# Fewer small routing steps on VectorE, placed only in the last two rounds of a top-k search, and GpSimd's row scaling ahead of its transfers

## The chip, the cores and the metric

The kernel runs on one core of one Trainium2 chip. The metric is the device time of that core in microseconds, from start to end of one execution; lower is better. The comparisons below use the median of several executions.

## The reference

Two blocks follow each other. The first is attention with 8 batches, 8 heads, 576 positions and 64 dimensions a head: of each row of scores only those not below the row's 32nd largest are kept. Its output is 4,608 tokens of 512 values. The second block sends each token to the one of 8 experts with the largest gate logit, runs it through that expert's two matrices (512 to 1,024, ReLU, 1,024 to 512) and scales it by the gate's probability.

```python
scores = scale * np.matmul(q, k.transpose(0, 1, 3, 2))
kth = np.partition(scores, -top_k, axis=-1)[..., -top_k:-top_k + 1]     # top_k = 32
attn = softmax(np.where(scores >= kth, scores, -1e9))
x = (attn @ v)                      # then (B,H,S,D) -> (B*S, H*D)
logits = x @ w_gate
expert_idx = np.argmax(logits, axis=1)
probs = softmax(logits)             # gate_w: the chosen expert's share
h = np.maximum(x_sorted[lo:hi] @ w1[e], 0.0)    # per expert e, tokens sorted by expert
y_sorted[lo:hi] = h @ w2[e]
out = gate_w[:, None] * y
```

## The kernel before, in words

**Attention.** A unit is two heads of one batch (u = 0 to 3), so a batch has four units. The work list has 144 steps, 18 a batch; each handles two tiles of 128 query rows against all 576 keys. One step goes through the engines in this way: TensorE multiplies queries and keys (line 292); ACT copies the scores from PSUM (L299); VectorE folds them in halves (L306, L308, and L314, L316 for the second fold) and searches for the 32 largest in four rounds, each of which takes the eight largest of either tile (MAX8, L354) and, but for the last, strikes them out (MATCH_REPLACE8, L362); ACT turns the 32nd largest into a bound (L371) and computes from it how far each score lies below it (L387); GpSimd subtracts that from the scores (L396, two instructions of 128x576 a step) and records doubts about the folding (L377); ACT takes the exponentials (L404); TensorE transposes the weights and multiplies by the values (L415 to L452). VectorE works on step i+1 while GpSimd subtracts for step i. A small instruction `nbias` (L358) on GpSimd follows round 0 of each search.

**After a unit** its output is brought into token order. The generator `ending` does that in pieces at named places of the loop. ACT forms divisors and VectorE their reciprocals (L481). At the place "rows" GpSimd multiplies the gate's partial logits (L489), adds them up (L491, L492, L494) and scales the rows (L502, 128x640).

**Routing** follows the last unit of a batch, while the next batch's attention runs. `choice` finds each token's expert (L512 to L522); TensorE counts the tokens before each (L533 to L536) and ACT copies the running count `run` (L1093); `places` turns that into row numbers `posi` and gate weights (L548 to L558); five indirect transfers on GpSimd's queue scatter the rows to DRAM (L569), one a step; `table` works out which experts have filled a block of 128 rows and lists the new blocks for the loader (L613 to L653). After batch 0, `filled_up` runs before `table`; in the last batch another table, `end_table`, and halves of blocks follow.

**The small steps of VectorE.** `choice`, `places`, `table` and the reciprocals are generators on a list `aside`. The search calls `tick()` between its instructions, and each call runs one small step:

```python
for m in m_all:
    nc.vector.max(out=tops[:, m, r * 8:(r + 1) * 8], in_=src[m])
    if r:
        tick()
```

The same stands behind each MATCH_REPLACE8, so rounds 1 and 2 have four places, round 3 has two. What is left on the list when the loop reaches a given place is run there in one go by `through`.

**Expert blocks** are cut in pieces of a few matmuls (L916, L933) that TensorE runs between the attention's products at a planned rate; ACT evacuates them (L813, L921, L942), and GpSimd's queue writes the results out by indirect transfers (`put_rows`, L831), collected in `stores`. A few blocks are kept back until attention has ended; the last ones (L852 to L892) need the last table.

**What sets the order.** TensorE, ACT and VectorE run in the order in which the program writes them. GpSimd's and SyncE's instructions are ordered by the scheduler that builds the kernel, from its own estimates, except that instructions put by `in_turn` keep their order among themselves; a scatter is also tied behind the last GpSimd instruction of the step that issued it. In each step of the loop, the scatter and the stores are issued just behind the subtraction and the doubts, before the places "pool", "relu" and "rows".

Of the kernel before, what the change touches and what calls it, by code (L numbers as in the profile page):

```python
# [9 lines left out]
F32 = mybir.dt.float32  # L10
# [9 lines left out]
NEG = -3.0e38  # L20
STEEP = 2.0 ** 120
EPS = 1e-9


def _ins(ap: bass.AP, axis: int, n: int) -> bass.AP:
# [12 lines left out]
def _inner(ap: bass.AP, n: int) -> bass.AP:  # L38
    return _ins(ap, len(ap.ap), n)
# [3 lines left out]
def kernel(  # L43
# [47 lines left out]
    nc = tc.nc  # L91
# [104 lines left out]
    nc.vector.tensor_copy(e_same, _ins(e_less[:, :], 1, KC))  # L196
    nc.vector.memset(e_same[ST:P, NC, :], 1.0)
    e_at = iota_f("e_at", [P, E], [[CAP, E]])
    slots = iota_f("slots", [1, NSLOT], [[1, NSLOT]])

    def token_ids(t, b):
        return nc.gpsimd.iota(t, pattern=[[P, KC]], base=b * S, channel_multiplier=1)
# [18 lines left out]
    slot_long = slot_last[:, 0, NSLOT + SOON - 3 * E:].rearrange("o (i e) -> o i e", i=3)  # L221
    assert LAST - SURE <= NSLOT + SOON - 3 * E
    done = const.tile([1, E], F32, name="done")
    nc.vector.tensor_scalar_mul(done, e_at[0:1, :], 1.0 / P)
    slot_max = const.tile([1, 3], F32, name="slot_max")
    rare = slot_max[:, 2:3]
    nc.vector.memset(slot_max[:, 0:1], float(E - 1))
    nc.vector.memset(slot_max[:, 1:2], float(EMPTY))
    upto_all = const.tile([1, E + 1], F32, name="upto_all")
    nc.vector.memset(upto_all, 0.0)  # L230
    step_all = const.tile([1, E], F32, name="step_all")
    nc.vector.memset(step_all, float(EMPTY))
# [100 lines left out]
    def search(tiles, s, f, then=lambda: None):  # L333

        m_all = range(2)
        tops = k.small.tile([P, 2, TOP_K], F32, name="tops", bufs=4)
        if k.exact:
            src = [s[:, m, :, :].rearrange("p j k -> p (j k)") for m in m_all]
            width = S
        else:  # L340
            src = [f.few[:, m, 0:QF] for m in m_all]
            width = LW
            for m in m_all:
                for j, away in enumerate((f.l[:, m, :], f.hl[:, m, 0:QF // 2], f.hl[:, m, QF // 2:QF])):
                    nc.vector.max(out=f.few[:, m, QF + 8 * j:QF + 8 * j + 8], in_=away)  # L345
        scr = k.att.tile([P, 2, width], F32, name="scr", bufs=1)
        nbias = k.small.tile([P, 2], F32, name="nbias", bufs=3)
        R = TOP_K // 8

        for r in range(R):  # L350
            if r == R - 1:
                then()
            for m in m_all:
                nc.vector.max(out=tops[:, m, r * 8:(r + 1) * 8], in_=src[m])  # L354
                if r:
                    tick()
            if r == 0:
                in_turn(nc.gpsimd.tensor_scalar_mul(nbias, tops[:, :, 0], -scale))  # L358
            if r < R - 1:
                for m in m_all:  # L360
                    first = r == 0 and not k.exact
                    nc.vector.match_replace(  # L362
                        out=src[m] if first else scr[:, m, :], in_to_replace=tops[:, m, r * 8:(r + 1) * 8],
                        in_values=src[m], imm_value=NEG,
                    )
                    if r:
                        tick()
                    src[m] = f.few[:, m, :] if first else scr[:, m, :]
        thr = tops[:, :, TOP_K - 1]
        low = k.small.tile([P, 2], F32, name="low", bufs=3)  # L370
        nc.scalar.activation(low, thr, AF.Copy, scale=STEEP)  # L371

        def doubts():
            n, i = tiles[0]
            at = n.b * U + n.u
            over = doubt[:, at:at + 2, 2 * NC, :] if tails(tiles) else doubt[:, at, 2 * i:2 * i + 2, :]
            k.last_pool = in_turn(nc.gpsimd.tensor_tensor(  # L377
                over, f.few[:, :, QF + 7:LW:8], _inner(thr, NL), op=ALU.subtract
            )).ins

        return low, nbias, doubts
# [122 lines left out]
    def choice(lg):  # L504
# [6 lines left out]
        def steps():  # L511
            nc.vector.tensor_reduce(mx, lg, axis=AX.X, op=ALU.max)  # L512
            yield
            nc.vector.tensor_tensor(oh, lg, _inner(mx[:, :], E), op=ALU.is_ge)
            yield
            nc.vector.tensor_tensor(oh, oh, _ins(e_less[:, :], 1, KC), op=ALU.mult)
            yield
            nc.vector.tensor_tensor(lg, lg, _inner(mx[:, :], E), op=ALU.subtract)
            yield
            nc.vector.tensor_reduce(idx, oh, axis=AX.X, op=ALU.min)  # L520
            yield
# [18 lines left out]
    def places(r, x):  # L540

        pos = k.small.tile([P, KC, E], F32, name="pos")
        posf = k.small.tile([P, KC], F32, name="posf")
        r.posi = k.small.tile([P, KC], I32, name="posi")
        den = k.small.tile([P, KC], F32, name="den")

        def steps():
# [1 line left out]
            yield  # L549
            nc.vector.tensor_reduce(den, r.lg, axis=AX.X, op=ALU.add)  # L550
            yield
            nc.vector.tensor_reduce(posf, pos, axis=AX.X, op=ALU.add)
            yield
            nc.vector.tensor_scalar_add(den, den, EPS)
            yield
            nc.vector.tensor_copy(r.posi, posf)
            yield
            nc.vector.reciprocal(x[:, :, Dm], den)  # L558
            yield
# [39 lines left out]
    def table(slot_i, n, last, riding=None):  # L599

        sm = k.small
        full = sm.tile([1, E], F32, name="full")
        ci = sm.tile([1, E], I32, name="ci")
        left = sm.tile([1, E], F32, name="left")
        past = sm.tile([1, NSLOT, E], F32, name="past", bufs=1)
        slot_f = sm.tile([1, 2, NSLOT], F32, name="slot_f", bufs=1)
        upto, step = upto_all, step_all

        def steps():
            if last:  # L610
                nc.vector.tensor_scalar_add(full, run[0:1, :], float(P - 1))
                yield
            nc.vector.tensor_copy(ci, full if last else run[0:1, :])  # L613
            yield
            nc.vector.tensor_single_scalar(ci, ci, 7, op=ALU.arith_shift_right)
            yield
            nc.vector.tensor_copy(full, ci)
            yield
            if riding is not None:
                nc.vector.tensor_tensor(full, full, riding, op=ALU.subtract)  # L620
                nc.vector.tensor_tensor(full, full, done, op=ALU.max)
                yield
            nc.vector.tensor_tensor(left, full, done, op=ALU.subtract)
            yield
            nc.vector.tensor_tensor_scan(upto[:, 1:], ones[0:1, 0:E], left, 0.0, op0=ALU.mult, op1=ALU.add)
            yield
            nc.vector.tensor_tensor(step[:, 0:E - 1], done[:, 1:E], full[:, 0:E - 1], op=ALU.subtract)
            yield
            nc.vector.tensor_tensor(
                past[:, 0:n, :], _inner(slots[:, 0:n], E), _ins(upto[:, 1:], 1, n), op=ALU.is_ge  # L630
            )
            yield
            nc.vector.tensor_reduce(slot_f[:, 0, 0:n], past[:, 0:n, :], axis=AX.X, op=ALU.add)
            yield
            nc.vector.tensor_tensor(past[:, 0:n, :], past[:, 0:n, :], _ins(step[:, :], 1, n), op=ALU.mult)
            yield
            nc.vector.tensor_reduce(slot_f[:, 1, 0:n], past[:, 0:n, :], axis=AX.X, op=ALU.add)
            yield
            nc.vector.scalar_tensor_tensor(
                out=slot_f[:, 1, 0:n], in0=slot_f[:, 1, 0:n], scalar=done[:, 0:1], in1=slots[:, 0:n],  # L640
                op0=ALU.add, op1=ALU.add,
            )
            yield
            nc.vector.tensor_tensor(slot_i[:, :, 0:n], slot_f[:, :, 0:n], _inner(slot_max[:, 0:2], n), op=ALU.min)
            yield
            if last:
                nc.vector.tensor_copy(rest_i, upto[:, E:])
            else:
                nc.vector.tensor_scalar_min(upto, upto, float(n))
                yield  # L650
                nc.vector.tensor_tensor(left, upto[:, 1:], upto[:, 0:E], op=ALU.subtract)
                yield
                nc.vector.tensor_tensor(done, done, left, op=ALU.add)  # L653
                yield

        return steps()
# [1 line left out]
    def filled_up():  # L658
# [3 lines left out]
        yield  # L662
        nc.vector.max(out=most, in_=few)
        yield
        nc.vector.tensor_scalar(few, few, most[:, SOON - 1:SOON], float(P), ALU.is_ge, ALU.mult)
        yield
        nc.vector.tensor_tensor(few, few, e_at, op=ALU.add)
        yield
        nc.vector.tensor_tensor(run, run, few, op=ALU.max)
        yield  # L670

    def counted():
# [287 lines left out]
    with fast:  # L960
# [84 lines left out]
        def ending(b, u):  # L1045
# [45 lines left out]
            aside.append(steps)  # L1091
            yield "relu"
            nc.scalar.copy(run, r.run)  # L1093
            yield "pool"
            through(steps)
            scatters.extend(scattering(r, x))
# [6 lines left out]
            if b == B - 1:  # L1103
                scatter(KC)
                slot_i = k.small.tile([1, 2, NSLOT], I32, name="slot_i")
                half, full = counted()
                through(table(slot_i, SURE, False, half))
                firsts = [(slot_i[0:1, 0, j:j + 1], slot_i[0:1, 1, j:j + 1]) for j in range(SURE)]
                ready = load_rows(SimpleNamespace(), firsts[0][1], True)
            new = LAST - SURE if b == B - 1 else new_of[b]  # L1110
# [51 lines left out]
        def loop():  # L1162
# [9 lines left out]
            for i, (b, g) in enumerate(work):  # L1172
# [13 lines left out]
                w_of[i] = depths(s_of[i], low)  # L1186
                less(s_of.pop(i), w_of[i])
                doubts()
                put_stores()
                scatter(1)  # L1190
                at_place("pool")
                at_place("relu")
                at_place("rows")
                at = i % per_batch
                if at == FIRST and b:
                    rate = level(b) * PIECES / (U * NT)
# [65 lines left out]
    with ExitStack() as outer:  # L1262
# [10 lines left out]
        with ExitStack() as st:  # L1273
# [2 lines left out]
            ids = keep.tile([P, KC], I32, name="ids")  # L1276
            token_ids(ids, 0)
            nc.vector.tensor_copy(run, e_at)
            nc.vector.tensor_scalar_mul(done, e_at[0:1, :], 1.0 / P)
            slot_d = dram.tile([2 * NSLOT, 1], I32, name="slot_d")  # L1280
            with tc.For_i(0, B, 1) as b:
                x = k.xp.tile([P, KC, XW], F32, name="x")
# [95 lines left out]
```

## Time and profile before

| what | value |
|---|---|
| median of 3 executions | 1325.49 us (1323.74 to 1325.93) |
| profiled execution | 1322.96 us, of which 1321.3 us span |
| TensorE busy (matmul) | 1194.3 us, 90% of the span |
| VectorE busy | 1072.6 us, 81% |
| ACT busy | 932.3 us, 71% |
| GpSimd busy | 660.2 us, 50% |
| mean granted TensorE clock | 0.961 of full speed |

The span is the time from the first to the last instruction in one profiled execution; what lies around it is 1.7 us. The shares are means over parts of the execution with different limits: attention runs up to about 1070 us, after which VectorE has almost nothing to do and TensorE works on the remaining expert blocks. The times of a step or an instruction below are from this one execution. An instruction's duration in the profile includes time in which it stood in its engine waiting for something that is no semaphore; such time does not appear as idle.

### The profile page before, as it was taken

What the parts mean: (1) busy time and instruction counts of PE and PEld (TensorE: products, weight loads), DVE (VectorE), ACT (ScalarE), POOL (GpSimd) and SP (SyncE); (2) the same over time, 40 slices, a digit from 0 to 9 for tenths busy, and PEclk for the clock granted to TensorE, in tenths of its full rate; (3) what the DMA queues carried; (4) which work ended last, traced back from release to release, by engine and by line L of the source; (5) the groups of instructions that cost most, each with busy time, mean ns of one, the idle gap of its engine ahead of it and who ended that gap; (6) DMA issues with size and microseconds to landing.
All of it is one profiled execution on the core that took longest, in us unless ns stands there. A gap on an engine that the chain in (4) does not pass through costs nothing. (4 is left out here: it accounts for less than half of the span.)

```text
span 1321.3 us, 24526 instructions
## 1 busy us (share of the span) xinstructions
PE 1194.3 (90%) x7654; PEld 838.0 (63%) x7654; DVE 1072.6 (81%) x4654; ACT 932.3 (71%) x2129; POOL 660.2 (50%) x806
## 2 busy tenths in 40 slices
PE   5767777898989899999999999999999999999995
PEld 3444444665666556666666666766676777699973
DVE  7999999999999999999999999999999943000000
ACT  4888878887898788888888888788878861111110
POOL 2454546554865485647564765575656642000000
PEclk9798887999999999999999999999999999999998
DMA  4000001841293029522955374447454659986580
GB/s 149 30 30 30 30 30 64 319 155 30 71 345 133 30 74 373 179 101 74 367 174 184 134 249 173 163 144 265 156 179 162 197 185 289 386 301 215 209 292 18
DMA packets 98509, 220.95 MB, mean 167 GB/s; under 512 B 5181, under 2 KB 25917, under 8 KB 98368
## 3 DMA queue, kind: packets, MB, share of 16 engines
q1 hardware_dynamic: 91664, 199.02, 43.1%
q0 software_dynamic: 6416, 19.97, 4.2%
q8 instruction: 62, 1.02, 0.3%
q14 instruction: 79, 0.65, 0.1%
q10 hardware_dynamic: 288, 0.30, 0.1%
HBM read 195.88 MB, written 24.17 MB: 167 GB/s over the span
## 5 line engine op out<-in xcount | busy, mean ns | idle before, releaser
L396 POOL TENSOR_TENSOR w<-s,w 128x576 f32<-128x576 f32 x288 | 410.5, 1445 | 412.8 <-ACT w L387 412.8
L916 PE MATMUL ph<-xTs,w 128*128 128x128 f32 x2112 | 261.2, 277 | 3.6 <-ACT xTs L813 3.6
L916 PEld LDWEIGHTS ph<-xTs,w 128*128 128x128 f32 x2112 | 249.6, 193 | 22.7 <-issue 18.0
L933 PE MATMUL py<-w,hT 128*128 128x512 f32 x528 | 249.6, 602 | 3.9 <-ACT hT L921 3.7
L404 ACT ACTIVATE w<-w,nbias 128x576 f32<-128x576 f32 x288 | 224.1, 792 | 4.8 <-POOL w L396 3.9
L387 ACT ACTIVATE w<-s,low 128x576 f32<-128x576 f32 x288 | 207.7, 768 | 4.7
L292 PE MATMUL sc<-qkb 64*128 64x288 f32 (+1 forms) x1280 | 200.7, 464 | 9.7 <-ACT s L299 5.1
L415 PE MATMUL wTm<-turn,w 128*128 128x128 f32 x1152 | 170.2, 288 | 32.1 <-ACT xl L470 15.8
L415 PEld LDWEIGHTS wTm<-turn,w 128*128 128x128 f32 x1152 | 133.3, 146 | 89.3 <-issue 32.3
L299 ACT COPY s<-sc 128x576 f32<-128x576 f32 x288 | 168.7, 639 | 10.0 <-PE sc L292 10.0
L1257 DVE CAST any_i<-pd 1x1 int32<-1x1 f32 x1 | 0.1, 146 | 201.1 <-PE pd L1255 201.1
L354 DVE MAX8 tops<-scr 128x8 f32<-128x168 f32 x576 | 163.1, 317 | 0.0
L422 ACT COPY wT<-wTm 128x512 f32<-128x512 f32 x256 | 139.1, 603 | 23.7 <-PE wTm L415 23.6
L354 DVE MAX8 tops<-few 128x8 f32<-128x144 f32 (+1 forms) x576 | 154.9, 301 | 0.0
L292 PEld LDWEIGHTS sc<-qkb 64*128 64x128 f32 (+1 forms) x1280 | 107.4, 191 | 71.0 <-issue 32.7
L933 PEld LDWEIGHTS py<-w,hT 128*128 128x128 f32 x528 | 92.4, 192 | 89.4 <-issue 83.5
L452 PE MATMUL po<-wT,vb 128*64 128x288 f32 x1024 | 148.1, 435 | 0.0
L345 DVE MAX8 few<-l 128x8 f32<-128x288 f32 x288 | 127.5, 443 | 0.0
L831 POOL DMA_INDIRECT out_dram<-y,xg x37 | 38.1, 1030 | 171.4 <-ACT y L892 76.5
L452 PEld LDWEIGHTS po<-wT,vb 128*64 128x64 f32 x1024 | 71.9, 145 | 71.8 <-issue 21.5
L306 DVE TENSOR_TENSOR h<-s 128x576 f32<-128x576 f32 x144 | 114.1, 792 | 2.5 <-ACT s L299 2.5
L308 DVE TENSOR_TENSOR l<-s 128x576 f32<-128x576 f32 x144 | 109.2, 758 | 0.0
(189 smaller groups left out, 1650.1 us busy)
## 6 DMA issues: line engine op xcount, KB each, us to landing
w<-in_moe_w_dram SPq DMA_DIRECT2D x74, 2048.0 KB, 9.2
qkb<-in_qk_dram SPq DMA_DIRECT2D x31, 608.0 KB, 4.0
vb<-in_v_dram SPq DMA_DIRECT2D x32, 320.0 KB, 3.3
xg<-x_rows SPq DMA_DIRECT2D x37, 257.0 KB, 9.1
x_rows<-blank SPq DMA_DIRECT2D x13, 257.0 KB, 5.4
x_rows<-blank POOLq DMA_DIRECT2D x4, 257.0 KB, 8.0
x_rows<-x,posi POOLq DMA_INDIRECT x40, 3.1
out_dram<-y,xg POOLq DMA_INDIRECT x37, 4.1
```

The source lines that it names most:

```text
L292: nc.tensor.matmul(ps[rows, j, 0:HF], n.q[d, cols], n.k[d, keys], start=True, stop=True)
L299: lambda m=m, ps=ps: nc.scalar.copy(s[:, m, :, :], ps[:, :, 0:HF]) for m, ps in enumerate(got)
L345: nc.vector.max(out=f.few[:, m, QF + 8 * j:QF + 8 * j + 8], in_=away)
L354: nc.vector.max(out=tops[:, m, r * 8:(r + 1) * 8], in_=src[m])
L387: nc.scalar.activation(w[:, m, :], s[:, m, :, :].rearrange("p j k -> p (j k)"), AF.Relu, scale=-STEEP, bias=low[:, m:m + 1],)
L396: k.last_pool = in_turn(nc.gpsimd.tensor_tensor(w[:, m, :], s[:, m, :, :].rearrange("p j k -> p (j k)"), w[:, m, :], op=ALU.subtract)).ins
L404: nc.scalar.activation(w[:, m, :], w[:, m, :], AF.Exp, scale=scale, bias=nbias[:, m:m + 1], accum_out=n.z[:, c:c + 1])
L415: nc.tensor.transpose(pm[:, c * P:(c + 1) * P], w[:, m, first:first + P], ident)
L422: nc.scalar.copy(wT[:, :, m, q], pm4)
L452: nc.tensor.matmul(po[r, 0:HF], n.v[:, c, r], rhs, start=(c == 0), stop=(c == KC - 1))
L916: nc.tensor.matmul(ph[:, f, :], n.w1[:, 0, dt, fc * P:(fc + 1) * P], n.xT[:, dt, :], start=(dt == 0), stop=(dt == DT - 1),)
L933: nc.tensor.matmul(py, hT[:, f, :], n.w2[:, 0, f, :], start=(f == 0), stop=(f == FT - 1))
```

## The change

It has four parts.

1. The routing's small steps are fewer. `choice` forms `lg - max` first and fuses the comparison with zero and the multiplication by `e_less` in one instruction. `places` lets the reduction write the integer positions itself. `table` no longer converts to integers, shifts and converts back: ACT writes `blocks`, the running count over 128 less a bit under a half, from PSUM, and adding and later subtracting 1.5 * 2^23 (`WHOLE`) rounds it to a whole number; the two reductions over `past` are one. Of `choice`, `places` and `table` together a batch has 22 small steps in the place of 27.
2. `tick()` is called only in rounds 2 and 3 of a search.
3. In a step of the loop, the stores and the scatter are issued behind the places "pool", "relu" and "rows" and no longer before them.
4. A few constants are added ahead of the first step (`e_up`, `slots_less`, `blocks`), and `done` carries `WHOLE` until the last batch takes it off.

The last table of the rare exact path (`last`) changes with it; that path is not run with these inputs.

```diff
@@ search
             for m in m_all:
                 nc.vector.max(out=tops[:, m, r * 8:(r + 1) * 8], in_=src[m])
-                if r:
+                if r > 1:
                     tick()
...
-                    if r:
+                    if r > 1:
                         tick()
@@ choice
             nc.vector.tensor_reduce(mx, lg, axis=AX.X, op=ALU.max)
             yield
-            nc.vector.tensor_tensor(oh, lg, _inner(mx[:, :], E), op=ALU.is_ge)
-            yield
-            nc.vector.tensor_tensor(oh, oh, _ins(e_less[:, :], 1, KC), op=ALU.mult)
-            yield
             nc.vector.tensor_tensor(lg, lg, _inner(mx[:, :], E), op=ALU.subtract)
+            yield
+            nc.vector.scalar_tensor_tensor(
+                out=oh, in0=lg, scalar=0.0, in1=_ins(e_less[:, :], 1, KC), op0=ALU.is_ge, op1=ALU.mult
+            )
             yield
@@ places
-            nc.vector.tensor_reduce(posf, pos, axis=AX.X, op=ALU.add)
+            with nc.allow_low_precision(reason="one whole number and zeros are added"):
+                nc.vector.tensor_reduce(r.posi, pos, axis=AX.X, op=ALU.add)
             yield
             nc.vector.tensor_scalar_add(den, den, EPS)
-            yield
-            nc.vector.tensor_copy(r.posi, posf)
             yield
@@ table
-            nc.vector.tensor_copy(ci, full if last else run[0:1, :])
-            yield
-            nc.vector.tensor_single_scalar(ci, ci, 7, op=ALU.arith_shift_right)
-            yield
-            nc.vector.tensor_copy(full, ci)
+            ...
+                v.tensor_scalar(full, blocks, WHOLE, None, ALU.add)
             yield
...
-            nc.vector.tensor_reduce(slot_f[:, 0, 0:n], past[:, 0:n, :], axis=AX.X, op=ALU.add)
-            yield
-            nc.vector.tensor_tensor(past[:, 0:n, :], past[:, 0:n, :], _ins(step[:, :], 1, n), op=ALU.mult)
-            yield
-            nc.vector.tensor_reduce(slot_f[:, 1, 0:n], past[:, 0:n, :], axis=AX.X, op=ALU.add)
+            v.tensor_tensor(second, first, _ins(step[:, :], 1, n), op=ALU.mult)
+            yield
+            v.tensor_reduce(slot_f[:, 1, 0:n] if last else slot_f[:, :, 0:n], both, axis=AX.X, op=ALU.add)
             yield
@@ ending
             nc.scalar.copy(run, r.run)
+            if b:
+                nc.scalar.activation(blocks, r.run[0:1, :], AF.Copy, scale=1.0 / P, bias=UNDER)
@@ ending, last batch
                 through(table(slot_i, SURE, False, half))
+                nc.vector.tensor_scalar_add(done, done, -WHOLE)
@@ loop
                 less(s_of.pop(i), w_of[i])
                 doubts()
-                put_stores()
-                scatter(1)
                 at_place("pool")
                 at_place("relu")
                 at_place("rows")
+                put_stores()
+                scatter(1)
```

In `filled_up`, which runs once, the comparison and the addition of `e_at` are likewise one instruction, and one is added that forms `blocks`.

## The prediction

> **What bounds the kernel now.** I read the stages first, then VectorE's groups, its timeline beside GpSimd's, and last who waits for whom. Busy time by stretch (us, then PE, PEld, DVE, ACT, POOL, clock, DMA share, GB/s):
>
> ```profile
> 33.00:165.00 132.00, 92.49 (x535) 55.57 (x535) 132.00 (x571) 108.89 (x255) 68.98 (x92) 0.84 0.09 30
> 165.00:540.00 375.00, 328.66 (x2125) 218.39 (x2127) 374.51 (x1638) 313.81 (x727) 226.21 (x269) 0.94 0.41 147
> 540.00:1070.00 530.00, 517.31 (x3504) 357.94 (x3501) 524.23 (x2244) 446.53 (x1031) 324.72 (x384) 1.00 0.52 183
> 1070.00:1110.00 40.00, 39.95 (x252) 28.82 (x251) 15.44 (x89) 13.52 (x33) 14.09 (x19) 1.00 0.66 224
> ```
>
> Up to 540 us VectorE is idle for 0.5 us in all, and TensorE has 46 us to spare from 165 us on: a microsecond off VectorE is a microsecond off the kernel. From 540 to 1070 both are nearly full: TensorE idles 12.7 us, so no more than that can come off there. After 1070 TensorE works through blocks that are ready; that part only moves.
>
> VectorE's timeline repeats every 6.94 us: eight MAX8 in four rounds, starting 0, 0.96, 2.04 and 3.85 us after the step's first. In an undisturbed step GpSimd's two L396 subtractions run from -1.39 to 1.45 us: over rounds 0 and 1, done before round 2. All else is excess over 6.94, read from the start of one step's first MAX8 to the next one's. It sums to 18.5 us of steps in 165 to 540 us. Most is small routing steps that stretch, as their groups show (duration min/median/max in ns, from the view of one line):
>
> ```profile
> L514 DVE TENSOR_TENSOR oh<-lg,mx x8: 175/594/1386, 169.7 to 1087.6; 128x40 f32<-128x40 f32 x8
> L512 DVE TENSOR_REDUCE mx<-lg x8: 171/174/197, 169.4 to 1087.4; 128x5 f32<-128x40 f32 x8
> L613 DVE CAST ci<-run x8: 141/548/1394, 198.9 to 1093.3; 1x8 int32<-1x8 f32 x8
> ```
>
> The same shape costs 175 or 1386 ns; the reduction beside it never varies. The timelines of GpSimd and VectorE over one such step show what it waits for:
>
> ```profile
> 297.69 2.77 POOL L396 TENSOR_TENSOR w<-s,w 128x576 f32<-128x576 f32 x2
> ...
> 298.80 0.18 DVE L512 TENSOR_REDUCE mx<-lg 128x5 f32<-128x40 f32 x1
> 298.89 0.33 DVE L354 MAX8 tops<-few 128x8 f32<-128x168 f32 x1
> 299.13 1.38 DVE L514 TENSOR_TENSOR oh<-lg,mx 128x40 f32<-128x40 f32 x1
> ```
>
> L514 ends at 300.51, just behind L396 (300.46). Mean minus minimum, times eight: L514 4.5, L613 4.1, L615 2.2, L516 1.9, L623 1.3, L625 and L518 1.1 and 1.0, others 2.4: 18.5 us. Row scaling (L502) does the same to the folds, depending on when it starts. First without, then with a transfer (L569) before it:
>
> ```profile
> 264.90 1.26 POOL L502 TENSOR_TENSOR x<-xl,rz 128x640 f32<-128x640 f32 x1
> ...
> 265.47 1.00 DVE L314 TENSOR_TENSOR few<-h 128x288 f32<-128x288 f32 x1
> ...
> 229.42 0.96 POOL L569 DMA_INDIRECT x_rows<-x,posi  x1 [0.15 <-issue]
> ...
> 232.02 2.49 POOL L502 TENSOR_TENSOR x<-xl,rz 128x640 f32<-128x640 f32 x1
> ...
> 232.00 0.73 DVE L306 TENSOR_TENSOR h<-s 128x576 f32<-128x576 f32 x1
> ```
>
> In the first case L314 loses 0.56 us (1.00 against 0.44). In the second L306 starts 0.02 us ahead, VectorE loses nothing and GpSimd takes twice as long. Last, waits of the stretch 540 to 1070 (PE) and of the span (DVE): us, times, longest.
>
> ```profile
> PE wTl L431 <- ACT wT L422: 6.3, 14, 1.1
> PE wTm L415 <- ACT oT L454: 1.7, 3, 0.8
> DVE rz L481 <- ACT rz L477: 9.0, 5, 5.7
> ```
>
> Four of those five waits for the divisors, and one for L479 (1.2 us), fall between 540 and 950: 4.5 us in the first tick of round 1.
>
> **The Trainium skill.** SBUF — State Buffer, "Who interferes with whom": VectorE instructions with two SBUF inputs, and copies, casts and scalar forms in their 2-port mode, exclude a GpSimd instruction; whoever issues first holds the pair for the whole instruction; reductions never contend. The lines above agree in each point (1386 against 175 ns; 171 to 197 ns; L502 at 1.26 or 2.49 us). VectorE: DVE Perf Modes, "Rules for kernel authors", says to minimize the count of operations. Here an undisturbed small step adds less than its duration: six of them (L512 to L522, 183 us) moved round 3 from 3.85 to 4.49, 0.107 us each.
>
> **The change, part by part.** (1) *Fewer small steps.* Choice goes from 6 to 5, places from 6 to 5, the table from 15 to 12: at 0.107 us some 0.5 us a batch. The fused is_ge-and-mult is not in the trace; its nearest rows are 183 ns (L516) and 250 ns (L639), so it costs between -0.1 and 0.1 us more than a plain one; I take 0. ACT gets `blocks`, like L476 at 190 ns, seven times: 1.3 us on an engine with over 60 us idle in the 375; behind it wait only the divisors, so nothing, and 0.2 us a batch if that slack were gone. The constants before the first step and one addition at the end of the last batch are hidden by loads and by TensorE's ready blocks; unhidden they cost 0.15 us each.
>
> (2) *Ticks only in rounds 2 and 3.* Six places a step instead of ten; in round 2 L396 is over in an undisturbed step. Choice, places with the next divisors, and the table's two halves need 5, 6, 6 and 6, so no further step is used. Where L396 is late the stall follows: at 298 us it ends 2.86 us into the step; the second small step, now at 2.63, waits 0.25 us instead of 1.2. The divisors are asked for 1.1 us later: the 4.5 us of waits and 0.5 us at 445 (L548) go. Next late is then ACT itself, which TensorE holds up.
>
> (3) *Rows ahead of transfers.* In the built order only five of 32 row scalings lose the transfer directly before them (17 stood behind one, 12 still do), all for the second pair of heads after a batch ends, since each scatter also moves one step earlier. By the traces above each now starts before L314 and costs 0.56 us that was free. For 11 of the 12, `nbias` (L358, 0.2 to 0.4 us) now stands ahead of the scaling. In the table's second step the scaling runs 4.3 to 5.6 us in, where today it costs L306 0.60; now small steps of round 3 stand there and wait some 1.0. The transfers' later place costs nothing: a scatter is one step earlier, a store at most 2.4 us later, and `y` has two buffers. SP's order changes in three places by one load; its landings have steps to spare, else TensorE would wait on DMA in the stretches above.
>
> Excess of the routing steps in us, before to after (choice, places, table 1, table 2, scaling of the second pair):
> - batch 0 (with `filled_up`): 0.66+0.56+0.56+1.76+0.46+0 = 4.00 to 0.53+0.52+0.50+1.50+0.60+0.56 = 4.21
> - batch 1: 1.86+0.56+1.36+1.06+0 = 4.84 to 0.80+0.50+0.60+1.50+0.56 = 3.96
> - batch 2: 1.86+1.16+1.96+1.06+0 = 6.04 to 0.80+0.50+0.95+1.50+0.56 = 4.31
>
> That is 2.4 us before 540, all on the path. After 540 the same working gives batches 3 to 6 +1.9, +0.7, -0.2 and +1.4, and the divisors 4.7 as step lengths: 8.5 us of VectorE. L396 is late there (starting up to 2.5 us into the step), so small steps in round 2 meet it still. TensorE has 12.7 us idle behind ACT; I take half of 8.5, 4.2 us, bounded by 0 and 8.5. Sum 6.6 us: the profiled execution goes from 1322.96 (span 1321.3 and 1.7 around it) to 1316.4; it lies 2.5 us under the median of 1325.49, which goes to 1318.9.
>
> **Rivals.**
> - *The port comes free altogether.* For: an undisturbed L396 ends 0.6 us ahead of round 2. Against: late L396 at 298, 428 and most routing steps after 690. Before 540 the stalls of batches 0 to 2 (4.9), count (1.5) and one wait (0.5), after it 60% of TensorE's 12.7: 14.5 us, 1311.0. Chance 0.15.
> - *TensorE binds after 540.* VectorE's gain there turns into idle time: 2.4 us or less, 1323.5. For: TensorE is at 97.6%. Against: ACT waits for VectorE's `tops` for 17 us in 600 to 1080. Chance 0.20.
> - *Slower: the collision moves and grows.* Row scaling and small steps now meet in rounds 2 and 3. If each of the two small steps that the table's second step has in round 3 waits for a GpSimd instruction of 1.4 us, that is 2.8 in place of 0.60 for L306, 2.2 more a batch, and with 0.56 for the second pair 8.3 us in batches 0 to 2 against 4.8 gained in the other steps; with nothing gained after 540 the kernel ends at 1329.0. It decides once these two places cost over 1.6 us a batch more than today; I put 0.44 and 0.56 in batches 1 and 2. For: L306 and L502 block each other there now. Against: L502 itself is 1.26 us and can block once. Chance 0.15.
> - *The reorder does nothing*, as 12 scalings stay behind transfers: my sum plus 1.7, within the main case.
>
> **The numbers.** Main case 1318.9, its own range 1315 to 1323, chance 0.50. A measurement here can tell about 0.2%, 2.65 us. Faster 0.65 (0.48 of the main case, all of the free port, 0.02 of TensorE's), same 0.22 (0.18 of TensorE's, 0.02 each of the main and the slower case), slower 0.13. The range reaches to 1311.5 for most of the free port and to 1326.5 for TensorE's case and part of the slower one.
>
> **What would show it.** Right: small two-input steps near 180 ns except by late L396; L481 without idle time; L314 at 1.0 us five times more; TensorE's idle time in 540 to 1070 at 8 to 9 us. Wrong: VectorE idle over 8 us in that stretch with TensorE as before (second rival), or round-3 small steps beyond 1.5 us (third).

## The result, and the profile after

The changed kernel is faster by half a per cent: median 1316.88 us (1314.10 to 1319.47, 4 runs) against 1324.70 us for the kernel before on the same chip, ratio 0.9944, 95% interval [0.9932, 0.9957]. Its profiled execution took 1319.47 us (span 1317.9), the slowest of the four. On two other chips the ratio was 0.9963 [0.9949, 0.9977] and 0.9950 [0.9936, 0.9963]. The forecast was 1318.9 us, 0.995 of the median shown.

The same stretches as before, in the same columns (us; PE, PEld, DVE, ACT, POOL busy; clock; DMA share; GB/s):

```profile
33.00:165.00 132.00, 93.14 (x534) 54.83 (x535) 132.00 (x571) 108.68 (x254) 70.17 (x92) 0.84 0.10 30
165.00:540.00 375.00, 327.31 (x2146) 218.02 (x2147) 375.00 (x1640) 315.11 (x735) 225.36 (x272) 0.96 0.42 150
540.00:1070.00 530.00, 520.77 (x3519) 359.94 (x3517) 521.37 (x2208) 449.51 (x1041) 329.90 (x386) 1.00 0.53 183
1070.00:1110.00 40.00, 39.95 (x253) 29.98 (x252) 13.93 (x83) 9.27 (x22) 12.21 (x16) 1.00 0.80 250
```

The picture of what binds is the old one: VectorE is full up to 540 us, TensorE nearly so after it. In the third row VectorE's 8.6 us of idle time is not a new wait: the last search now ends at 1062.10 us instead of 1069.51, and 6.7 us of the idle time lie behind it; before that end it fell from 5.3 to 1.9 us. The changed small steps in the view of one line (duration min/median/max in ns; L519, L521 and L626 stand where L512, the late two-input step and the table's first step stood):

```profile
L519 DVE TENSOR_REDUCE mx<-lg x8: 169/172/196, 170.5 to 1079.9; 128x5 f32<-128x40 f32 x8
L521 DVE TENSOR_TENSOR lg<-lg,mx x8: 172/317/1009, 170.9 to 1080.2; 128x40 f32<-128x40 f32 x8
L626 DVE TENSOR_SCALAR full<-blocks x8: 140/266/1353, 199.7 to 1085.9; 1x8 f32<-1x8 f32 x8
```

The medians fall from 594 to 317 ns and from 548 to 266, the maxima from 1386 to 1009 and from 1394 to 1353: such an instruction is stretched less often, but can still be stretched about as far. The step that showed it best before (298 us) now reads, on VectorE and GpSimd:

```profile
298.09 2.77 POOL L403 TENSOR_TENSOR w<-s,w 128x576 f32<-128x576 f32 x2
...
300.25 0.18 DVE L519 TENSOR_REDUCE mx<-lg 128x5 f32<-128x40 f32 x1
...
300.58 0.34 DVE L521 TENSOR_TENSOR lg<-lg,mx 128x40 f32<-128x40 f32 x1
```

L403 (L396 before) ends at 300.86, and the two-input step waits 0.16 us for it instead of 1.2. The price stands at the second pair of heads, where the row scaling (L509, before L502) has lost the transfer ahead of it and starts before the fold L321 (before L314):

```profile
230.04 1.26 POOL L509 TENSOR_TENSOR x<-xl,rz 128x640 f32<-128x640 f32 x1
...
230.62 0.99 DVE L321 TENSOR_TENSOR few<-h 128x288 f32<-128x288 f32 x1
```

Last the waits (us, times, longest), of TensorE between 540 and 1070 us, then of VectorE over the span:

```profile
PE wTl L438 <- ACT wT L429: 5.2, 11, 1.1
```

```profile
DVE rz L488 <- ACT rz L484: 5.7, 1, 5.7
...
DVE rz L488 <- ACT rz L486: 1.6, 1, 1.6
```

Four of the five waits for divisors are gone, and the 1.2 us one has become 1.6. TensorE's idle time from 540 us to the last search's end goes from 12.7 to 9.2 us.

### The profile page after: what moved, and what is told of

The parts are those of the page before. It is cut to its first block, busy times and chain, and to the rows that moved or that the text cites. A ratio compares the mean times of both kernels' runs of the same rounds, so it can differ in the third digit from the quotient of the medians.

```text
span 1317.9 us, 24504 instructions
## 1 busy us (share of the span) xinstructions
PE 1191.3 (90%) x7654; PEld 836.6 (63%) x7654; DVE 1069.2 (81%) x4617; ACT 931.7 (71%) x2136; POOL 662.0 (50%) x807
## 5 line engine op out<-in xcount | busy, mean ns | idle before, releaser
L403 POOL TENSOR_TENSOR w<-s,w 128x576 f32<-128x576 f32 x288 | 407.3, 1434 | 405.5 <-ACT w L394 405.4
L422 PE MATMUL wTm<-turn,w 128*128 128x128 f32 x1152 | 166.9, 284 | 22.8 <-ACT xl L477 11.0
L422 PEld LDWEIGHTS wTm<-turn,w 128*128 128x128 f32 x1152 | 130.4, 144 | 79.7 <-issue 33.6
L361 DVE MAX8 tops<-few 128x8 f32<-128x144 f32 (+1 forms) x576 | 151.0, 300 | 0.0
L313 DVE TENSOR_TENSOR h<-s 128x576 f32<-128x576 f32 x144 | 109.3, 759 | 2.0 <-ACT s L306 2.0
L315 DVE TENSOR_TENSOR l<-s 128x576 f32<-128x576 f32 x144 | 108.6, 754 | 0.0
```

The lines of the kernel that those rows point to most:

```text
L403: k.last_pool = in_turn(nc.gpsimd.tensor_tensor(w[:, m, :], s[:, m, :, :].rearrange("p j k -> p (j k)"), w[:, m, :], op=ALU.subtract)).ins
L422: nc.tensor.transpose(pm[:, c * P:(c + 1) * P], w[:, m, first:first + P], ident)
```

## The experiments

All gains are read as in the prediction: the excess of a step over 6.94 us, from one first MAX8 to the next one's. (An undisturbed step is 6.92 us to the hundredth, so it shows as -0.02; the prediction read its steps to 0.1 us.) Two marks are used below: the start of step 70 (batch 3, step 16), which has the routing of three batches behind it, and the end of the last search. Each run has its kernel before on the same chip: a median of 1324.70 us for the first profile, 1322.84 to 1323.31 in the three groups after it. The marks come from one profiled execution of each kernel, the medians from 4 to 21 executions.

| kernel | median us (range) | ratio, 95% | step 70 starts | last search ends |
|---|---|---|---|---|
| before | 1323.1 | 1 | 517.2 | 1069.5 |
| changed (first profile) | 1316.88 (5.4) | 0.9944 [0.9932, 0.9957] | 514.3 | 1062.1 |
| changed, second group (e0_after) | 1317.37 (6.5) | 0.9963 [0.9949, 0.9977] | 514.2 | 1060.4 |
| changed, third group (e8_after2) | 1317.20 (5.0) | 0.9950 [0.9936, 0.9963] | 518.6 | 1065.9 |
| fewer steps alone (e5_count) | 1321.88 (2.8) | 0.9990 [0.9982, 0.9998] | 517.1 | 1067.3 |
| ticks alone (e1_ticks) | 1319.17 (2.9) | 0.9970 [0.9958, 0.9982] | 516.6 | 1065.0 |
| reorder alone (e2_order) | 1332.26 (8.4) | 1.0071 [1.0054, 1.0088] | 521.1 | 1075.1 |
| changed, ticks from round 1 (e4_round1) | 1324.81 (3.1) | 1.0016 [1.0010, 1.0023] | 521.2 | 1071.0 |
| changed, no reorder (e3_no_order) | 1314.21 (1.8) | 0.9930 [0.9917, 0.9944] | 512.8 | 1060.8 |
| the same again (e9_no_order2) | 1314.48 (2.7) | 0.9937 [0.9923, 0.9950] | 512.5 | 1060.6 |
| changed, no reorder, scaling halved (e7_halves) | 1314.89 (1.3) | 0.9942 [0.9929, 0.9955] | 513.2 | 1061.3 |
| changed, blank stores moved (e6_fills) | 1321.43 (6.8) | 0.9991 [0.9982, 0.9999] | 518.2 | 1064.5 |

The figure in brackets behind a median is the distance from the fastest to the slowest run. Later ticks with the reorder but without fewer steps were not run.

**The changed kernel again (e0_after).** No edit.

> The changed kernel once more, to see how much of its spread comes from the tail. Port theory (small two-input steps waited for GpSimd's instruction, and now meet it less often): VectorE's last search ends 7.4 us before that of the kernel before, in every execution. Tail theory (a weight load after attention lands behind its use when attention ends earlier): executions differ by up to 4 us in the tail alone, so single times lie between 1314 and 1320 and the profile shows either a TensorE wait for a weight load of about 2 us near 1121 us or none. If the spread came from attention instead, the end of the last search would move between profiles by more than 1 us.

Its profiled execution, at 1314.0 us, was the fastest of the five. The end of attention moved by 1.7 us against the first profile, nearly all of it from step 70 to step 75 (2.84 us of excess there, and 1.21 here), so attention has a share in the spread. The rest lies in the tail. From the last search to TensorE's last matmul this execution needs the 236.6 us that every other profile here needs; the first profile needed 240.56. TensorE's timeline of that first profile and the stretch around it show why:

```profile
1123.62 9.01 PE L926 MATMUL ph<-xTs,w 128*128 128x128 f32 x64 [2.08 <-DMA w<-in_moe_w_dram]
```

```profile
1120.00:1130.00 10.00, 7.92 (x46) 6.79 (x45) 0.00 (x0) 1.28 (x2) 1.01 (x1) 0.83 1.04 401
```

A weight load of 2 MB that SyncE issued 44.67 us after the last search landed 61.38 us after it, 2.1 us later than its matmul was due (59.28). In five others, of the kernel before among them, it was issued at 42.6 to 42.9 and landed at 58.0 to 58.9, 0.4 to 1.3 us ahead. The wait costs 2.08 us, and a clock of 0.83 over the 10 us around it another 1.7, by estimate from these two figures: nearly all of the 3.9. So the first profile understates what attention gained.

**Without the reorder (e3_no_order).**

```diff
                 less(s_of.pop(i), w_of[i])
                 doubts()
+                put_stores()
+                scatter(1)
                 at_place("pool")
                 at_place("relu")
                 at_place("rows")
-                put_stores()
-                scatter(1)
```

> The changed kernel with stores and scatters issued ahead of the row scaling again (fewer steps and ticks in rounds 2 and 3 kept). Port theory: the second pair's row scaling stands behind its scatter again, starts after L306 and costs VectorE nothing: five steps lose 0.56 us each, 1.7 us of them before 540 us, so the last search ends 2 to 2.5 us earlier than in the changed kernel (near 1065) and the time is about 2 us less. Order theory (the reorder carries the gain): the last search ends 3 us or more later than in the changed kernel.

It beats both kernels: by the medians it is 3.2 us below the changed one in the same group. The second pair's steps (30, 48, 66) have no excess again, where the changed kernel has 0.53 to 0.54 in each of them. But its last search ends 0.4 us later than that of e0_after, the fastest of its five: the 2 to 2.5 us that the theory asked for do not show between these two profiles. Step 26 is 0.9 us shorter without the reorder, and step 126 is 1.8 us longer: with the reorder its subtractions begin at 0.42 us and are over before the folds; here they begin 2.45 us into the step, and both second folds wait for them:

```profile
932.41 2.99 POOL L403 TENSOR_TENSOR w<-s,w 128x576 f32<-128x576 f32 x2 [4.24 <-ACT w L394]
...
933.07 1.06 DVE L321 TENSOR_TENSOR few<-h 128x288 f32<-128x288 f32 x1
934.06 1.66 DVE L323 TENSOR_TENSOR hl<-h 128x288 f32<-128x288 f32 x1
```

**Ticks from round 1 in the changed kernel (e4_round1).**

```diff
-                if r > 1:
+                if r:
                     tick()
...
-                    if r > 1:
+                    if r:
                         tick()
```

> The changed kernel with ticks in rounds 1 to 3 again (22 small steps and the reorder kept). Port theory: small two-input steps of round 1 meet the subtraction L396 again; choice steps go back to 1.8 us of excess and first table steps to 1.3 to 1.9, the divisors' waits return, so the last search ends 4 to 6 us later than in the changed kernel, 1 to 3 us ahead of before. Count theory (22 steps in place of 27 carry the gain): the last search ends within 1 us of the changed kernel's, near 1067.

It falls behind the kernel before. The choice and table steps meet the late subtraction again (1.43 and 1.52 us of excess in the choice steps of batches 1 and 2, 2.01 and 2.06 in the table's first steps), and the table's second steps grow to 2.29 and 2.30. There VectorE and GpSimd read:

```profile
334.25 1.25 POOL L509 TENSOR_TENSOR x<-xl,rz 128x640 f32<-128x640 f32 x1
334.57 1.56 DVE L313 TENSOR_TENSOR h<-s 128x576 f32<-128x576 f32 x1
...
335.76 1.62 POOL L403 TENSOR_TENSOR w<-s,w 128x576 f32<-128x576 f32 x1 [0.25 <-ACT w L394]
336.05 1.95 DVE L315 TENSOR_TENSOR l<-s 128x576 f32<-128x576 f32 x1
```

Both folds of the next search pay: L313 waits for the row scaling (1.56 against 0.73 us), and by then the subtraction is there and L315 waits for that (1.95 against 0.75).

**Ticks alone, on the kernel before (e1_ticks).** The opposite edit of lines L355 and L366, with 27 steps a batch.

> The kernel before with one edit: ticks in rounds 2 and 3 only (27 small steps, old order). The table's 15 steps have 12 places, so three run in one go behind a search. Port theory: choice steps fall from 1.86 to about 0.9 us of excess, divisors no longer wait, the second pair's scaling stays free: the last search ends 5 to 7 us before that of the kernel before (1068 to 1070), 0.3 to 0.5% less time. Count theory: within 1 us of before.

A gain of 0.3%, or 3.7 us of the median, but in the profile only 0.6 us of it comes by step 70; 2.8 us come after step 73, where the waits for divisors are gone. Choice (0.73 and 0.76) and the table's first steps (0.43 and 1.10) improve; the table's second steps take back nearly all of it, at 3.02 and 3.06. A step now has six places; the table's last steps come in one go at its end, and there a subtraction has begun:

```profile
333.13 0.15 DVE L651 TENSOR_TENSOR left<-upto_all 1x8 f32<-1x8 f32 x1
333.16 1.41 POOL L396 TENSOR_TENSOR w<-s,w 128x576 f32<-128x576 f32 x1 [0.16 <-ACT w L387]
333.32 1.27 DVE L653 TENSOR_TENSOR done<-done,left 1x8 f32<-1x8 f32 x1
```

**The reorder alone, on the kernel before (e2_order).**

```diff
                 less(s_of.pop(i), w_of[i])
                 doubts()
-                put_stores()
-                scatter(1)
                 at_place("pool")
                 at_place("relu")
                 at_place("rows")
+                put_stores()
+                scatter(1)
```

> The kernel before with one edit: stores and scatters issued behind the row scaling (27 small steps, ticks in rounds 1 to 3). Port theory: the second pair's scaling now blocks L314, 0.56 us in five steps, and the table's second step pays for a scaling that starts later; about 3 us lost before 540 us, the last search ends 1 to 3 us later than in the kernel before (near 1071.5) and the time is 0 to 0.25% longer. Order theory (rows ahead of transfers free GpSimd earlier and gain): the last search ends 2 us or more earlier.

Slower by 0.7%, well beyond what was expected. By step 70 it has lost 3.9 us, most of it in the two places named: 0.54 to 0.56 in each second pair, and in the table's second steps 1.55 and 2.39 (1.07 and 1.08 before), the latter by the same pair of late folds as in the lines of e4_round1. Its profiled execution, at 1328.92 us, is 3.3 us faster than its median, so what the slower executions lose was not seen.

**Fewer steps alone (e5_count).** The changed kernel's `choice`, `places` and `table` with the old `tick()` and the old order.

> The kernel before with the small steps reduced to 22 and nothing else. Port theory: a step that meets no GpSimd instruction is worth 0.107 us, so 0.5 us a batch and about 2 us before the last search ends, and stalls stay (their number is set by where the remaining two-input steps fall): end 1067 to 1070. Count theory: 4 us or more earlier, end at 1065 or below.

1.2 us by the medians, and 0.1 us by step 70. Alone, five steps a batch are worth little: what is left still meets the late subtraction (1.70 at step 58, 2.07 at step 61).

**All blank stores on GpSimd's queue (e6_fills).** This takes 257 KB stores off SyncE, ahead of the late weight load.

```diff
-            on = nc.gpsimd if e % 2 else nc.sync
+            on = nc.gpsimd
```

> The changed kernel with one edit in the tail: all eight stores of blank rows (fill_up) on GpSimd's queue and none on SyncE's, so that the weight loads behind them on SyncE are issued sooner. Tail theory: that load is issued about 38 to 40 us after the last search in place of 43 to 45, lands 3 us or more ahead of its use at 59.3, no TensorE wait there in the profile; single times spread over less than 3 us, in place of 6, and the median falls to about 1314 to 1315. If the spread comes from elsewhere: spread and median as for the changed kernel, 1317.

The load was issued 37.72 us after the search and landed 2.4 us ahead of its use, as wanted. But the median was 1321.43 us (1317.23 to 1323.99, 13 runs), ratio 0.9991 [0.9982, 0.9999]: slower than the changed kernel, and no narrower. So the late load is not all that spreads the times. The loss has two parts in the profile. Behind TensorE's last matmul this execution takes another 18.6 us, where all others here take 15.1 to 15.6: that comes with the edit. And step 26 has 4.90 us of excess, where the first two profiles of the changed kernel have 1.79 and 1.77: that lies in attention, which the edit does not touch.

**Row scaling in two halves, without the reorder (e7_halves).**

```diff
-        in_turn(nc.gpsimd.tensor_tensor(xu, xl, _inner(rzb, D), op=ALU.mult))
+        for h in range(2):
+            in_turn(nc.gpsimd.tensor_tensor(
+                xu[:, :, h, :], xl[:, :, h, :], _inner(rzb[:, :, h], D), op=ALU.mult
+            ))
```

> The changed kernel in the old order of stores and scatters (as in e3_no_order), and with the row scaling cut in two GpSimd instructions of half the width, so that the port pair is given up half-way. Port theory (an instruction holds the pair to its end): L314 waits for the first half only, under 0.2 us in place of 0.56; nine such steps before 540 us and the collisions of the table's second step: the last search ends 2 to 5 us ahead of e3_no_order's (1056 to 1059), time 1310 to 1313. If what L314 waits for were something else than the one instruction, such as a queue of GpSimd's work: no change, 1314, or slower by the eight more fixed costs a batch on GpSimd.

1314.89 us (1314.45 to 1315.73), last search at 1061.3: nothing gained on e3_no_order. VectorE slips between the halves, and the second half then holds up the next fold instead of the first:

```profile
264.15 1.62 POOL L510 TENSOR_TENSOR x<-xl,rz 128x320 f32<-128x320 f32 x2
...
264.72 0.47 DVE L321 TENSOR_TENSOR few<-h 128x288 f32<-128x288 f32 x1
265.12 0.97 DVE L323 TENSOR_TENSOR hl<-h 128x288 f32<-128x288 f32 x1
```

**The spread: both again, side by side (e8_after2, e9_no_order2).** No edit to either.

> The changed kernel a third time, beside the kernel without the reorder on the same chip. If the reorder costs what the earlier runs say, its median is 2 to 4 us above the one without it and its times lie at least 4 us apart; if that difference was one of chips or of the hour, the two medians lie within 1 us. End of the last search in the profile: 1060 to 1065 us.

> The changed kernel without the reorder again. If the reorder costs time: ratio to before near 0.993, times within 2 us, last search ending at 1060.8 within 1 us. If not: ratio near 0.995 like the changed kernel's, with its spread.

The medians are 2.7 us apart, as forecast if the reorder costs time, and the ranges are 5.0 and 2.7 us; the second is wider than expected. This profile of the changed kernel caught the bad case, with 4.52 us of excess in step 26:

```profile
201.87 0.26 POOL L501 TENSOR_TENSOR lg<-xl 128x40 f32<-128x40 f32 x1
201.97 4.16 DVE L643 TENSOR_TENSOR past<-past,step_all 1x24 f32<-1x24 f32 x1
...
202.09 1.25 POOL L509 TENSOR_TENSOR x<-xl,rz 128x640 f32<-128x640 f32 x1
203.31 2.76 POOL L403 TENSOR_TENSOR w<-s,w 128x576 f32<-128x576 f32 x2
206.03 1.50 POOL L384 TENSOR_TENSOR doubt<-few,tops 128x6 f32<-128x6 f32 x1
206.06 0.74 DVE L313 TENSOR_TENSOR h<-s 128x576 f32<-128x576 f32 x1
```

L643 has 24 elements. It was due while L501 ran, and then got nothing through the row scaling and two subtractions, which follow one another without a gap; it ends 0.06 us after the last of them. This is the exception. In the same execution L626, of 8 elements, begins to wait under the first of two subtractions, which also follow each other without a gap, and gets in at the end of that first one (859.39 us):

```profile
857.97 2.78 POOL L403 TENSOR_TENSOR w<-s,w 128x576 f32<-128x576 f32 x2 [6.92 <-ACT w L394]
...
858.07 1.34 DVE L626 TENSOR_SCALAR full<-blocks 1x8 f32<-1x8 f32 x1
```

In the twelve profiles a VectorE instruction was waiting 85 times as the first of two such subtractions ended: 83 times it came before the second, and twice it did not, the L643 of e8_after2 and the L643 of e6_fills. Both had begun to wait under L501, as had a fold of e4_round1 at 873.55 us, which stayed out through the row scaling behind it. Whether L501 makes the difference, and why, is open.

In e0_after the same GpSimd instructions are spaced differently and L638, one small step earlier, pays 1.37 us. Without the reorder, GpSimd still has the scatter ahead; the scaling and L643 start within 0.01 us of each other, and it is the scaling that waits:

```profile
202.22 2.63 POOL L509 TENSOR_TENSOR x<-xl,rz 128x640 f32<-128x640 f32 x1
202.23 0.15 DVE L643 TENSOR_TENSOR past<-past,step_all 1x24 f32<-1x24 f32 x1
...
202.31 0.74 DVE L313 TENSOR_TENSOR h<-s 128x576 f32<-128x576 f32 x1
```

Here GpSimd waits, 2.63 us for an instruction of 1.25, and VectorE loses nothing. Set side by side, four executions of the changed attention (first profile, e0, e8, e6) and two without the reorder add 27.3 to 27.6 us of excess each from the start of step 76 to that of step 126; up to step 76 they differ, in few places: step 26 (1.79, 1.77, 4.52, 4.90 against 0.86 and 0.83), the second pairs, step 61, and steps 70 to 75.

## Why the prediction was right, and where it was not

**The table by batch.** The terms, worked out from one trace, came close in most places (excess in us, sums of the same five or six steps; three profiles of the changed kernel in order, then e3_no_order):

| | before | forecast | changed | e3_no_order |
|---|---|---|---|---|
| batch 0 | 3.92 | 4.21 | 4.25, 4.26, 6.98 | 2.85 |
| batch 1 | 4.85 | 3.96 | 3.76, 3.77, 3.77 | 3.17 |
| batch 2 | 6.02 | 4.31 | 3.65, 3.64, 4.86 | 4.24 |

The second pair's 0.56 came as priced (0.53 to 0.54), three times before 540 us. The table's second step, set at 1.50, measured 1.58 to 1.60 in batches 1 and 2 of all three. The 4.86 of batch 2 comes from the table's first step, 1.71 for the 0.95 forecast.

**A reading that was wrong.** The prediction has 18.5 us twice, and they are not the same. The first is the excess of the steps between 165 and 540 us. The second adds up how far small steps stretch over the whole execution, to 1094 us; between 165 and 540 us they stretch by 5.5 us, and the folds by 6.2. So small steps were not most of what could be won there. The forecast was built on the table by batch and did not suffer from it.

**The mis-sized term** is the table's second step in batch 0: 1.50 forecast, 1.79, 1.77 and 4.52 measured. What failed is the argument against the slower rival, that row scaling "is 1.26 us and can block once". It looked at one GpSimd instruction at a time; in e8_after2 a VectorE instruction stayed out through the scaling and two subtractions behind it, 4.1 us. The Trainium skill (SBUF — State Buffer, "Who interferes with whom") states that whoever issues first holds the pair for the whole instruction. The traces agree for a single one (L626 above waits 1.2 us, to the end of the first subtraction). They show besides that the waiting side comes next nearly always, 83 times in 85, but not always.

**Before 540 us** I forecast 2.4 us. By step 70 the changed kernel is ahead by 2.9 and 3.0 us in two profiles and behind by 1.4 in the third.

**After 540 us** I let the path take 4.2 of 8.5 us. From the first MAX8 of step 73 to the last search's end it was 529.4 us before and 524.9, 524.5 and 524.9 after: 4.5 to 5.0. The half was a choice, and that it came out right in sum is luck. The routing of batches 3 to 5, forecast to gain 2.4 us, gained nothing in steps 76 to 125 (27.0 us of excess, then 27.5). Steps 73 to 75 bring 1.3 to 1.8 us and steps 127 to the end 1.8; there steps 73 and 127 lose their waits for divisors. The other 2.0 us are step 126, where the reorder lets the subtractions start early, which I had not forecast.

**The sum** was 6.6 us. The last search ends 7.4, 9.1 and 3.6 us earlier. The profiled execution was to take 1316.4 us; the three took 1319.47, 1314.0 and 1319.4, the first with 3.9 us lost behind attention, in a part that I had said "only moves". That it moves onto a load with 0.4 us to spare was in the trace, and the prediction left it out.

**The signs I named.** TensorE's idle time from 540 to 1070 us, forecast at 8 to 9 us, was 9.2, 8.9 and 9.3, at the upper edge or past it. VectorE idle over 8 us in that stretch was to speak for the second rival, "with TensorE as before"; it was 8.6 in the first profile, but 6.7 of it lie behind the last search and TensorE was not as before. L488 (L481) still has one wait: 1.58 us at 644 us, where step 87 is longer than before (2.53 against 1.32). The fold L321 is over 0.8 us in 22 cases (11 before), including the second pairs at 230, 360, 489 and 758 us; I had counted five more in all and not followed the late ones.

**The rivals.** The port (the access that VectorE and GpSimd share) did not come free: from 165 to 1070 us small steps stretch by 14.6 us in the first profile after, 18.2 before, but the folds by 29.8, 21.9 before (durations less the shortest of each group). TensorE did not swallow the gain after 540. The slower case is real as a mechanism: the reorder alone is 0.7% slower, and the two places named make up most of its loss up to step 70.

**What carries the gain.** By the medians fewer steps alone bring 1.2 us and later ticks alone 3.7, but both together, without the reorder, 8.6 and 8.8. The difference is made early: by step 70 it is 0.1 us and 0.6 us alone, and 4.4 together. The trace of e1_ticks shows a reason: 15 table steps don't fit the 12 places of two rounds, and the rest collides (3.02 and 3.06 us in the table's second steps of batches 1 and 2); 12 fit (1.59 and 1.60 in e3_no_order). The prediction noted that "no further step is used" but added the parts up as if independent. The reorder costs 2.7 to 3.2 us of the median in the two groups that ran both, although it gains 1.3 to 1.8 us after step 73 (526.2 and 526.3 us without it). All of that gain is step 126: its excess is -0.02 or -0.01 in every profile with the reorder and 1.8 to 2.0 in every one without. ACT is late there without it, after a wait of 1.9 us for TensorE's `px` in step 125 that is 0.3 us with it; I have not followed it further back.

**Open.** What decides between the two cases of step 26 is not shown. The difference is there a step earlier: in step 25 ACT waits for TensorE's `po` 1.8 and 1.7 us in the two mild profiles and 2.7 and 3.2 us in the two bad ones, and the subtractions, and GpSimd's work behind them, come later by about as much. Without the reorder that wait is 3.1 us and VectorE loses nothing to the scaling, as the scatter still stands ahead of it. Why TensorE is late was not traced. The 1.05 us at step 70 occurs in the kernel before too, and the uneven steps up to 72 with it, so they are not the change's.

## What to carry to other kernels

Small steps and the places free of the other engine have to be counted together: thinning the steps out brought 0.1% and moving them 0.3%, and both together 0.6 to 0.7%, because only then did they fit. When an instruction of a sharing engine loses what stood ahead of it, ask what it now runs back to back with: here a stall went through three instructions in a row in two of four profiles of one change, though in most places the waiting side came next. The changed kernel's times spread over 5 to 6.5 us, and its profiles differ in a few steps only: where times spread, several profiles of the same kernel, compared step by step, tell more than one.

## What was not expected of the hardware

- A VectorE instruction of 24 elements took 4.16 us behind GpSimd's L501, L509 and two L403 in a row (e8_after2, and likewise e6_fills); undisturbed it takes 0.15. Yet 83 of 85 VectorE instructions that waited under the first of two such subtractions came before the second.
- Halving a GpSimd instruction moved a stall of about 0.5 us from one fold to the next and took none away (e7_halves).
- After a 2.08 us wait of TensorE the granted clock was 0.83 in that 10 us stretch, where it was 1.00 in the undisturbed execution. This was seen once, and that the wait lowered the clock is not shown.
